# Loading k and v by one 128-partition DMA with three tokens per run, and the difference of the choice in SBUF

## The chip, the cores and the metric

The kernel runs on one core of one Trainium2 chip. The metric is the device time of one execution in microseconds. Engines are named as in the profile: PE (matmul) and PEld (its weight loads), DVE, ACT, POOL, and SP, which issues most of the DMAs.

## The reference

Attention with normalised q and k over 8 batches of 12 heads, 448 tokens and a head width of 64, then a routed layer of 8 experts on the 3584 tokens.

```
q_n, k_n = rmsnorm(q, g_q), rmsnorm(k, g_k)
attn = softmax(q_n @ k_n.T / 8)            # per head, 448 x 448
x = (attn @ v) as (3584, 768)
y_dense = relu(x @ w1_dense) @ w2_dense
logits = x @ w_gate                        # 8 experts
e = argmax(logits); gate = softmax(logits)[e]
out = y_dense + gate * (relu(x @ w1[e]) @ w2[e])
```

All inputs are float32; the matmuls are done in bfloat16.

## The kernel before, in words

**Groups and periods.** The work of attention is cut into 24 groups of four heads (two pairs; three groups make a batch). `first()` fills the pipeline, then `period(g)` (L663) runs once for each of 23 groups, and `final()` ends attention and runs the expert stage (32 tiles of 128 tokens with gathered records). The order of all engines' work is written out by hand: `PLAN` (L642) lists, for each of the three groups of a batch, short names that `period` turns into calls. Each engine works through its instructions in that order.

**What a group goes through.** `load` (L196) brings q, k and v of a group to SBUF; q and k are issued in period g for group g+5 (`Lq`, `Lk`), v for group g+4 (`Lv`). `squares` (L225) squares q and k, on POOL for all but the first groups (L239); `sums` (L241) adds the squares on DVE (L244); `norms` (L248) makes 1/rms on ACT; `normalise` (L271) multiplies, q and half of k on DVE (L285, L282), the other half of k on POOL (L279). `transposes` (L287) turns them on PE (L295), and `turned` (L298) copies the result on DVE (L301 for q, L306 for k). `values` (L219) casts v to bfloat16 on POOL (L221), with a column of ones behind each half. `scores` (L309) does q times k on PE (L319) and the exponential on ACT (L321). `single` (L323, L335) and `attend` (L339, L344) multiply the exponentials with v; `divide` (L348) divides on DVE. `xtrans` (L359, L365) turns the result on PE for the layer that follows. In period g, squares are made for group g+3 and normalising is done for g+2.

**Layout of k and v.** A pair of heads has 7 slots of 64 columns. Slots 0 to 2 are the first head on 128 partitions, slots 4 to 6 the second head, and slot 3 holds the first head's rest on partitions 0 to 63 and the second head's rest on 64 to 127. So 448 tokens of each head are 3.5 slots. Before, this is loaded by four DMAs (L215): for each of the two heads of a pair 256 tokens, four in a run of 1,024 bytes, onto one half of the partitions, and 192 tokens, three in a run of 768 bytes, onto the other half; each DMA covers both pairs. q is loaded by one DMA (L208) of 128 partitions with seven tokens in a run (1,792 bytes), since its slots are permuted back later.

**Buffers and queues.** The q and k buffers (`lds`, three groups deep, L177) lie in the memory of the last two experts' weights, which are loaded when the last groups are done with them; in the profile these loads are `we<-in_q_dram` and `we<-in_k_dram`. v has two buffers (`xv`). SP issues the loads in order q, k, v. In `first()`, ACT's queue issues the second head's pieces of k for groups 0 and 1, ahead of ACT's table load (L749). As the program is built, the loads of SP and ACT use eight completion semaphores in turn, so every load waits until the eighth load before it has landed. The weights go by POOL's queue (`weights`, L631), a few per period, and so do the records of routed tokens (`scatter`, L590).

**The choice of an expert.** Once per batch `logits` (L374) writes 32 numbers a partition to PSUM, and `choose` (L384) picks the largest on DVE: the maximum (L390), the difference to it (L391, into PSUM), a product of "difference is zero" and a priority (L392), its maximum (L395), and the comparison that gives the one-hot choice (L397). `egates` (L407) takes the exponential of the difference on ACT (L409), from PSUM; `gates` (L411) sums and inverts. The PSUM tile is the one that `single` opens anew in the next group (L335).

`lanes` (L152) is some small constant work in `first()` that goes back and forth between DVE (L155 to L160) and POOL (L157, L158).

Of the kernel before, what the change touches and what calls it, by code (L numbers as in the profile page):

```python
# [9 lines left out]
F32 = mybir.dt.float32  # L10
# [3 lines left out]
ALU = mybir.AluOpType  # L14
# [4 lines left out]
def kernel(  # L19
# [14 lines left out]
    nc = tc.nc  # L34
    P = 128
    B, H, S, D = q.shape
    N = B * S
    Dm = H * D
    E = moe_w_gate.shape[1]
    F = moe_w1_dense.shape[1]  # L40
    J = 7
# [7 lines left out]
    De = D + 2  # L49
# [113 lines left out]
    with tc.tile_pool(name="a_ld", bufs=2) as ld, \  # L163
# [13 lines left out]
        lds = [lflat[:, i * 4 * S:(i + 1) * 4 * S].bitcast(F32) for i in range(6)]  # L177
# [18 lines left out]
        def load(g, names="qkv"):  # L196
            if g >= NG:
                return
            for name in names:
                src = dict(q=q, k=k, v=v)[name].rearrange("b h s d -> (b h) s d")[4 * g:4 * g + 4]  # L200
                if name == "v":
                    x = ld.tile([P, 2 * J * D], F32, tag="xv", name="xv")
                else:
                    x = lds[g % 3 * 2 + "qk".index(name)]
                xin[name, g] = x
                xi = x.rearrange("p (i s) -> p i s", i=2)
                if name == "q":
                    nc.sync.dma_start(xi, src.rearrange("(i r) (p j) d -> (r p) i (j d)", r=2, j=J))  # L208
                    continue
                heads = src.rearrange("(i r) s d -> r i s d", r=2)  # L210
                for r in range(2):
                    for c, s0, half in ((4, 0, r), (3, 4 * D, 1 - r)):
                        eng = nc.scalar if g < 2 and name == "k" and r else nc.sync
                        o = (0 if r == 0 else J - c) * D
                        eng.dma_start(xi[half * D:(half + 1) * D, :, o:o + c * D],  # L215
                                      heads[r, :, s0:s0 + c * D]
                                      .rearrange("i (p c) d -> p i (c d)", c=c))
# [7 lines left out]
        def squares(g, name, scalar=False, hs=slice(0, 2)):  # L225
            if (name, g) not in sqs:
                if g == 2:

                    n = "qk".index(name) * 2 * J * D
                    sqs[name, g] = (rall[:, 8:12].rearrange("p m c -> p (m c)")  # L230
                                    [:, n:n + 2 * J * D])
                else:
                    sqs[name, g] = sb.tile([P, 2 * J * D], F32, tag="sq", name="sq", bufs=2)
            o = slice(hs.start * J * D, hs.stop * J * D)
            x, y = xin[name, g][:, o], sqs[name, g][:, o]
            if scalar:
                nc.scalar.activation(y, x, AF.Square)  # L237
            else:
                nc.gpsimd.tensor_mul(y, x, x)  # L239
# [31 lines left out]
        def normalise(g, name, part):  # L271
# [4 lines left out]
            x = xin[name, g].rearrange("p (h j d) -> p h j d", h=2, d=D)  # L276
# [46 lines left out]
        def single(g, hh):  # L323
# [8 lines left out]
            for m in range(4):  # L332
                for r in range(GP):
                    rows = slice(r * D, (r + 1) * D)
                    nc.tensor.matmul(av[:, r, m], exs[g, 3][rows, hh, QC[m]:QC[m] + P],  # L335
                                     vabs[g % 3][rows, hh * J + 3, :De], start=(m == 0), stop=False,
                                     skip_group_check=True)

        def attend(g, hh, ms):  # L339
            av = avs[hh][:, :, :4 * De].rearrange("p r (m e) -> p r m e", e=De)  # L340
            for m in ms:
                for r in range(GP):
                    for j in range(4 * r, 4 * r + 3):
                        nc.tensor.matmul(av[:, r, m], exs[g, j][:, hh, QC[m]:QC[m] + P],  # L344
                                         vabs[g % 3][:, hh * J + j, :De], start=False,
# [38 lines left out]
        def choose(b):  # L384

            ws = trs["w"]
            lp, hot, cent = [ws[:, i * 4 * E:(i + 1) * 4 * E].rearrange("p (m e) -> p m e", e=E)
                             for i in range(3)]
            mx = sb.tile([P, 4, 1], F32, tag="mx", name="mx")
            nc.vector.tensor_reduce(mx, lp, AX.X, ALU.max)  # L390
            nc.vector.tensor_sub(cent, lp, mx.to_broadcast([P, 4, E]))  # L391
            nc.vector.scalar_tensor_tensor(hot, in0=cent, scalar=0.0,  # L392
                                           in1=prio, op0=ALU.is_equal, op1=ALU.mult)
# [599 lines left out]
```

## Time and profile before

| what | value |
|---|---|
| three runs | 401.67, 404.77, 410.85 us |
| median | 404.77 us |
| the profiled execution | 403.7 us, its span 402.0 us |
| PE busy | 341.9 us (85%) |
| PEld, DVE, ACT, POOL busy | 201.2, 225.2, 223.6, 212.3 us |
| DMA | 80.43 MB in 93,493 packets |
| mean granted clock of PE | 0.958 |

Times in the profile are microseconds from the start of the span; in rows of groups the mean is in ns. A row of the timeline has its start, its length, the engine, the line of the code, the operation, what it writes and reads, and how many were merged; square brackets show how long the engine stood idle before it and what ended that. A row of a wait has the sum of the idle time, how often, and the longest. In rows of stretches, DMA share is the busy time of the sixteen DMA engines over the length of the stretch; it can pass 1 a little where packets overlap.

### The profile page before, as it was taken

What the parts mean: (1) busy time and instruction counts of PE and PEld (TensorE: products, weight loads), DVE (VectorE), ACT (ScalarE), POOL (GpSimd) and SP (SyncE); (2) the same over time, 40 slices, a digit from 0 to 9 for tenths busy, and PEclk for the clock granted to TensorE, in tenths of its full rate; (3) what the DMA queues carried; (4) which work ended last, traced back from release to release, by engine and by line L of the source; (5) the groups of instructions that cost most, each with busy time, mean ns of one, the idle gap of its engine ahead of it and who ended that gap; (6) DMA issues with size and microseconds to landing.
All of it is one profiled execution on the core that took longest, in us unless ns stands there. A gap on an engine that the chain in (4) does not pass through costs nothing. (4 is left out here: it accounts for less than half of the span.)

```text
span 402.0 us, 10379 instructions
## 1 busy us (share of the span) xinstructions
PE 341.9 (85%) x3737; PEld 201.2 (50%) x3799; DVE 225.2 (56%) x455; ACT 223.6 (56%) x353; POOL 212.3 (53%) x222
## 2 busy tenths in 40 slices
PE   7589779789789788887988997999999999989940
PEld 3245545445455545544555564455555555545520
DVE  4689779769778777787788553712121212212210
ACT  4579858768778768678868752323233332322300
POOL 6686485966885776577887413544522121211220
PEclk9989989899999989899989998999999999999995
DMA  8979989999998989787999899999867867657530
GB/s 213 239 179 221 243 205 231 248 262 235 277 241 207 255 223 243 244 185 235 232 219 238 190 209 198 202 236 213 214 153 156 195 126 127 138 130 189 133 118 0
DMA packets 93493, 80.43 MB, mean 200 GB/s; under 512 B 53754, under 2 KB 84986, under 8 KB 93440
## 3 DMA queue, kind: packets, MB, share of 16 engines
q1 hardware_dynamic: 81360, 43.45, 49.7%
q0 software_dynamic: 11504, 35.81, 35.5%
q8 instruction: 34, 0.56, 0.6%
q10 hardware_dynamic: 576, 0.46, 0.4%
q14 instruction: 19, 0.16, 0.1%
HBM read 61.40 MB, written 26.19 MB: 218 GB/s over the span
## 5 line engine op out<-in xcount | busy, mean ns | idle before, releaser
L321 ACT ACTIVATE exf<-sc 128x896 bf16<-128x896 f32 x168 | 150.4, 916 | 47.7 <-PE sc L319 43.0
L239 POOL TENSOR_TENSOR sq<-we 128x896 f32<-128x896 f32 (+1 forms) x43 | 72.3, 1682 | 8.7 <-DMA we<-in_q_dram 3.2
L319 PE MATMUL sc<-T 64*128 64x448 bf16 (+1 forms) x384 | 63.4, 375 | 15.4 <-ACT exf L321 12.5
L591 POOL DMA_INDIRECT records<-rall,slot x32 | 33.0, 1032 | 47.4 <-issue 12.7
L853 ACT COPY heT<-hp 128x512 bf16<-128x512 bf16 x32 | 18.7, 586 | 66.7 <-PE hp L851 66.7
L244 DVE TENSOR_REDUCE ssq<-sq 128x14 f32<-128x896 f32 (+1 forms) x48 | 49.6, 1039 | 8.2 <-ACT sq L237 4.3
L344 PE MATMUL av<-va,exf 128*128 128x66 bf16 x1152 | 53.5, 197 | 0.0
L870 DVE COPY exf<-yp 128x768 f32<-128x768 f32 x20 | 19.2, 958 | 59.1 <-PE yp L864 52.7
L871 POOL DMA_INDIRECT out_dram<-exf,tail x20 | 19.6, 979 | 55.0 <-DVE exf L870 55.0
L344 PEld LDWEIGHTS <-exf 128*128 128x128 bf16 x1152 | 41.8, 99 | 12.3 <-issue 9.7
L839 PE MATMUL he<-we,exf 128*128 x177 | 44.3, 385 | 3.5 <-DMA exf<-records 1.6
L859 PE MATMUL yp<-wd,exf 128*128 128x384 bf16 x256 | 46.8, 326 | 0.0
L864 PE MATMUL yp<-we,heT 128*128 x256 | 46.8, 326 | 0.0
L319 PEld LDWEIGHTS <-T 64*128 64x128 bf16 (+1 forms) x384 | 17.9, 96 | 54.0 <-issue 47.0
L609 PE MATMUL ff<-wd,xT 128*128 128x512 bf16 x117 | 41.3, 398 | 1.0 <-issue 0.3
L844 ACT ACTIVATE hs<-he,tail 128x512 bf16<-128x512 f32 x32 | 22.0, 687 | 27.0 <-PE he L839 22.8
L859 PEld LDWEIGHTS <-exf 128*128 128x128 bf16 x256 | 25.0, 98 | 19.7
L354 DVE TENSOR_TENSOR rall<-av,inv 128x512 bf16<-128x512 f32 x48 | 33.2, 692 | 1.7
L870 DVE COPY rall<-yp 128x768 f32<-128x768 f32 x12 | 11.5, 958 | 39.5 <-PE yp L864 39.5
L864 PEld LDWEIGHTS <-heT 128*128 128x128 bf16 x256 | 25.0, 98 | 16.6
L279 POOL TENSOR_TENSOR xn<-we,r 128x448 bf16<-128x448 f32 x25 | 23.8, 953 | 16.0 <-ACT r L269 9.8
L871 POOL DMA_INDIRECT out_dram<-rall,tail x12 | 11.8, 979 | 35.4 <-DVE rall L870 35.4
(160 smaller groups left out, 441.9 us busy)
## 6 DMA issues: line engine op xcount, KB each, us to landing
we<-in_moe_w_dram POOLq DMA_DIRECT2D x16, 768.0 KB
we<-in_q_dram SPq DMA_DIRECT2D x24, 448.0 KB
xv<-in_v_dram SPq DMA_DIRECT2D x48, 128.0 KB
we<-in_k_dram SPq DMA_DIRECT2D x46, 128.0 KB
xv<-in_v_dram SPq DMA_DIRECT2D x48, 96.0 KB
we<-in_k_dram SPq DMA_DIRECT2D x46, 96.0 KB
wd<-in_moe_w_dense_dram POOLq DMA_DIRECT2D x2, 768.0 KB
exf<-records SPq DMA_TRANSPOSE x64
```

What stands on the lines that cost most here:

```text
L239: nc.gpsimd.tensor_mul(y, x, x)
L244: nc.vector.tensor_reduce(ssqs[g][:, "qk".index(name), hs], sqs[name, g].rearrange("p (h j d) -> p h j d", h=2, d=D)[:, hs], AX.X, ALU.add)
L319: nc.tensor.matmul(ps[o, hh, :S], kT[rows, j * P + o.start:j * P + o.stop], qT[rows, r * S:(r + 1) * S], start=True, stop=True)
L321: nc.scalar.activation(x, ps[:, :, :S], AF.Exp, scale=scale)
L344: nc.tensor.matmul(av[:, r, m], exs[g, j][:, hh, QC[m]:QC[m] + P], vabs[g % 3][:, hh * J + j, :De], start=False, stop=(j == 4 * r + 2), sk ...
L354: nc.vector.tensor_mul(xas[b].rearrange("p m a c -> p (m a) c")[:, :, o:o + D] .rearrange("p n (r d) -> p r n d", r=2), av[:, :, :, :Dh], ...
L591: i = nc.gpsimd.indirect_dma_start(out=rec, out_offset=bass.IndirectOffsetOnAxis(ap=slot[b % 2][:, m:m + 1], axis=0), in_=rb[b % 3][:, m], ...
L609: nc.tensor.matmul(ff[0], xTs[b][:, kk, QC[m]:QC[m] + P], wd1[:, kk], start=(kk == 0), stop=(kk == KD - 1))
L839: nc.tensor.matmul(he, xRs[t][:, kk % 2 * 5 + kk // 2], we[:, :n][:, bass.ds(eregs[t], 1), 0, kk * F:(kk + 1) * F] .rearrange("p o f -> p ...
L859: nc.tensor.matmul(yp[:, dd, :HD], xRs[t][:, i // 2 * 5 + 3 + i % 2], wd2[:, i, dd * HD:(dd + 1) * HD], start=(i == 0), stop=False)
L864: nc.tensor.matmul(yp[:, dd, :HD], heTs[t][:, i], we[:, :EA if t < KA else E][:, bass.ds(eregs[t], 1), 1, i * Dm + dd * HD:i * Dm + (dd + ...
L871: i = nc.gpsimd.indirect_dma_start(out=out, out_offset=bass.IndirectOffsetOnAxis(ap=tail[:, t, 1:2], axis=0), in_=ys.rearrange("p a d -> p ...
```

## The change

k and v are loaded by three DMAs in place of four. One covers 128 partitions and takes the first 384 tokens of all four heads, three in a run (768 bytes, four runs a partition). Two small ones cover 64 partitions each and take the last 64 tokens of each head, one in a run (256 bytes), into the shared slot. All are issued by SP, the first groups' too. For that, k's buffer grows from 14 to 16 slots, with one unused slot behind each pair, so that k is read as two runs of 448 numbers; v's slots are put in another order, the four heads' three slots first and the shared ones last, and `vslot` gives the matmuls the place. In `choose` the difference goes to a tile in SBUF, and "is the largest" is found by comparing the logits with the maximum, in an operation of its own before the product with the priority: six DVE operations in place of five. ACT takes the exponential from the SBUF tile.

```diff
-        lds = [lflat[:, i * 4 * S:(i + 1) * 4 * S].bitcast(F32) for i in range(6)]
+        WQ, WK = 2 * J * D, 16 * D
+        lds = [lflat[:, 2 * o:2 * (o + w)].bitcast(F32) for i in range(3)
+               for o, w in ((i * (WQ + WK), WQ), (i * (WQ + WK) + WQ, WK))]
...
                 if name == "v":
-                    x = ld.tile([P, 2 * J * D], F32, tag="xv", name="xv")
+                    x = ld.tile([P, WQ], F32, tag="xv", name="xv")
+                    xin[name, g] = x
+                    a, c = x[:, :12 * D], x[:, 12 * D:].rearrange("p (i d) -> p i d", i=2)
                 else:
                     x = lds[g % 3 * 2 + "qk".index(name)]
-                xin[name, g] = x
-                xi = x.rearrange("p (i s) -> p i s", i=2)
+                    xi = x.rearrange("p (i s) -> p i s", i=2)
+                    xin[name, g] = xi[:, :, :J * D]
+                    a, c = x, xi[:, :, 3 * D:4 * D]
...
-                heads = src.rearrange("(i r) s d -> r i s d", r=2)
+                nc.sync.dma_start(a.rearrange("p (n x) -> p n x", n=4)[:, :, :3 * D],
+                                  src[:, :3 * P].rearrange("n (p c) d -> p n (c d)", c=3))
                 for r in range(2):
-                    for c, s0, half in ((4, 0, r), (3, 4 * D, 1 - r)):
-                        eng = nc.scalar if g < 2 and name == "k" and r else nc.sync
-                        o = (0 if r == 0 else J - c) * D
-                        eng.dma_start(xi[half * D:(half + 1) * D, :, o:o + c * D],
-                                      heads[r, :, s0:s0 + c * D]
-                                      .rearrange("i (p c) d -> p i (c d)", c=c))
+                    nc.sync.dma_start(c[r * D:(r + 1) * D],
+                                      src[:, 3 * P:].rearrange("(i r) p d -> r p i d", r=2)[r])
+
+        def vslot(i, j):
+            return 12 + i if j == 3 else 6 * i + j - j // 4
...
-            o = slice(hs.start * J * D, hs.stop * J * D)
-            x, y = xin[name, g][:, o], sqs[name, g][:, o]
+            x = xin[name, g][:, hs]
+            y = sqs[name, g].rearrange("p (h s) -> p h s", h=2)[:, hs]
...
-                                     vabs[g % 3][rows, hh * J + 3, :De], start=(m == 0), stop=False,
+                                     vabs[g % 3][rows, vslot(hh, 3), :De], start=(m == 0), stop=False,
...
-            lp, hot, cent = [ws[:, i * 4 * E:(i + 1) * 4 * E].rearrange("p (m e) -> p m e", e=E)
-                             for i in range(3)]
+            lp, hot = [ws[:, i * 4 * E:(i + 1) * 4 * E].rearrange("p (m e) -> p m e", e=E)
+                       for i in range(2)]
+            cent = sb.tile([P, 4, E], F32, tag="cent", name="cent", bufs=1)
...
-            nc.vector.scalar_tensor_tensor(hot, in0=cent, scalar=0.0,
-                                           in1=prio, op0=ALU.is_equal, op1=ALU.mult)
+            nc.vector.scalar_tensor_tensor(hot, in0=lp, scalar=0.0, in1=mx.to_broadcast([P, 4, E]),
+                                           op0=ALU.add, op1=ALU.is_equal)
+            nc.vector.scalar_tensor_tensor(hot, in0=hot, scalar=1.0, in1=prio, op0=ALU.mult,
+                                           op1=ALU.mult)
```

4 lines of the change are left out of this document (2 added, 2 removed).

## The prediction

> **What bounds the kernel now.** I read the page's header and DMA rows first, then the busy times by stretch, then SP's timeline and waits, and last the timeline around each stall of TensorE.
>
> ```profile
> span 402.0 us, 10379 instructions
> q1 hardware_dynamic: 81360, 43.45, 49.7%
> q10 hardware_dynamic: 576, 0.46, 0.4%
> ```
>
> ```profile
> 30.00:130.00 100.00, 84.65 (x1275) 52.43 (x1291) 82.55 (x152) 78.84 (x124) 69.98 (x61) 0.97 1.01 237
> 130.00:200.00 70.00, 58.77 (x854) 35.62 (x869) 53.48 (x99) 53.37 (x87) 51.73 (x47) 0.95 0.92 230
> 257.00:380.00 123.00, 120.70 (x756) 70.68 (x770) 29.20 (x38) 36.96 (x59) 36.34 (x38) 1.00 0.77 171
> ```
>
> The columns are length, busy PE, PEld, DVE, ACT, POOL, clock, DMA share and GB/s. The expert stage (257 to 380) is PE's own: 120.70 of 123 us busy; nothing in this change touches it. In the attention stage PE is busy 143.4 of 170 us, and the sixteen DMA engines are full (1.01 and 0.92) at only 230 to 237 GB/s. So there is no slack in the DMA engines, but a late load costs time only where PE ends up waiting for it. I looked for these places.
>
> First place, the start:
>
> ```profile
> 9.26 0.51 SPq L208 DMA_DIRECT2D we<-in_q_dram  x1
> 13.98 1.68 POOL L239 TENSOR_TENSOR rall<-we 128x896 f32<-128x896 f32 x1 [3.29 <-DMA we<-in_q_dram]
> 16.14 0.16 DVE L159 TENSOR_REDUCE lw<-lw 128x1 f32<-128x8 f32 x1 [2.03 <-POOL lw L158]
> 16.34 1.00 DVE L160 TENSOR_SCALAR lane<-lane,lw 128x8 f32<-128x8 f32 x1
> 17.25 1.07 DVE L285 TENSOR_TENSOR xn<-we,tq 128x896 bf16<-128x896 f32 x1
> 18.91 0.55 PE L295 MATMUL tq<-ident,xn 128*128 128x128 bf16 x7 [2.68 <-DVE xn L282]
> ```
>
> The third q (group 2) is issued at 9.26, POOL squares it at 13.98 after 3.29 us of waiting, the small lane work queues behind that on POOL, DVE stands 2.03 us for it, and PE stands 2.68 us for DVE. Second and third place, groups 5 and 6:
>
> ```profile
> 38.81 1.67 POOL L239 TENSOR_TENSOR sq<-we 128x896 f32<-128x896 f32 x1 [3.23 <-DMA we<-in_q_dram]
> 42.25 0.61 PE L365 MATMUL tx<-ident,rall 128*128 128x128 bf16 x8 [0.56 <-DVE T L301]
> 49.19 1.68 POOL L239 TENSOR_TENSOR sq<-we 128x896 f32<-128x896 f32 x1 [2.65 <-PE av L344]
> 50.91 1.09 DVE L244 TENSOR_REDUCE ssq<-sq 128x14 f32<-128x896 f32 x1 [3.26 <-POOL sq L239]
> 51.91 0.68 DVE L301 TENSOR_SCALAR T<-tq,gqk 128x896 bf16<-128x896 bf16 x1
> 52.64 0.61 PE L365 MATMUL tx<-ident,rall 128*128 128x128 bf16 x8 [3.21 <-DVE T L301]
> ```
>
> At 49.19 the row names PE, but a square reads only the loaded q and writes a free buffer; I take the wait to be q of group 6, issued at 40.01 (below). The chain is square, sum (3.26 us), the turned copy queued behind the sum on DVE, and PE stands 3.21 us.
>
> **Why those loads are late.** SP's queue and its waits between 30 and 280 us:
>
> ```profile
> 29.23 0.54 SPq L208 DMA_DIRECT2D we<-in_q_dram  x1
> 29.88 3.12 SPq L215 DMA_DIRECT2D we<-in_k_dram  x4
> 33.09 6.18 SPq L215 DMA_DIRECT2D xv<-in_v_dram  x4
> 39.32 0.59 SPq L719 DMA_DIRECT2D records<-rall  x1
> 40.01 0.38 SPq L208 DMA_DIRECT2D we<-in_q_dram  x1
> ```
>
> ```profile
> SPq L215 <- DMA we<-in_q_dram: 14.6, 8, 3.7
> ```
>
> A group is nine DMAs, and each waits for the eighth before it; so the last piece of v waits for q of its own group. That is the 6.18 us at 33.09, the 14.6 us in eight waits, and it holds q of group 6, whose buffer DVE had freed some 7 us earlier, until 40.01.
>
> And the transfers are slow when they are halves:
>
> ```profile
> 8.00:9.00 1.00, 0.52 (x3) 0.29 (x2) 1.00 (x3) 0.33 (x2) 1.00 (x2) 1.00 1.13 194
> 9.00:10.00 1.00, 0.66 (x9) 0.52 (x9) 0.69 (x3) 0.65 (x4) 0.46 (x2) 1.00 1.13 247
> 10.00:11.00 1.00, 0.58 (x7) 0.26 (x6) 0.80 (x2) 1.00 (x2) 0.69 (x1) 1.00 1.22 193
> 11.00:12.00 1.00, 0.74 (x8) 0.25 (x5) 0.65 (x2) 0.35 (x1) 0.00 (x0) 1.00 0.86 288
> 17.00:18.00 1.00, 0.00 (x0) 0.00 (x0) 1.00 (x2) 0.09 (x1) 1.00 (x2) 1.00 0.93 291
> 47.00:49.00 2.00, 2.00 (x43) 1.56 (x42) 0.64 (x2) 1.86 (x3) 0.00 (x0) 1.00 1.10 207
> ```
>
> From 8 to 11 and 47 to 49 pieces of k and v (64 partitions each) are in flight: full engines, 193 to 247 GB/s, mean of the four rows 210. At 11 to 12 and 17 to 18, some 2 us after a q was issued, mostly q (128 partitions) is: 288 and 291.
>
> **The change, part by part.**
>
> *Transfer of k and v.* A load stays 458,752 bytes. Now 512 packets of 768 and 1,024 bytes; then 512 of 768 and 256 of 256. If halves are the cause, it goes from 458,752/210 = 2.2 us to 458,752/290 = 1.6 us. If the shorter runs are (q's are 1,792 bytes), 50% more packets make it 3.3 us. The q10 row decides: ACT's four early pieces of k are packets of the same 768 and 1,024 bytes, and 0.46 MB took 0.4% of 16 times 402 us, 25.7 us, which is 17.9 GB/s an engine or 286 GB/s on sixteen. So such packets are not slow in themselves, and I take 1.6 us, plus 0.1 to 0.3 for the small ones.
>
> *Issue on SP.* Seven DMAs in place of nine per group. A q took 0.51 and four pieces 2.55 us (0.64 each); I take 0.5 to 0.65 for the big one, as q is the nearest, and 0.64 for a small one: 1.9 for 2.55 us. If 512 runs took twice a q's time it is 2.3, still less. The eighth DMA before now lies in the group before, so v no longer waits for its own q. ACT loses four issues; its table load moves up, which hides behind the wait for the first q. SP takes over the two early halves of k, so the second q is issued about 0.5 us later, covered by engines that still have k of group 0 to move.
>
> *The start.* Up to its third q 2.75 MB have to land. Three q at 290 and three k or v at 1.7 us are 4.7 + 5.1 = 9.8 us against 13.98 - 1.9 - 0.8 = 11.3 us in which they came (first bytes at 1.9 and 0.8 from the last byte to its use, read from the trace's packet records, which no view lists). That is 1.5 us; with SP issuing that q near 7.8, and the second k no longer held for a semaphore, I take 1.9, between 1.0 and 2.6. PE's 2.68 us there cover all of it.
>
> *Groups 5 and 6.* q of group 5 is issued 3 to 5 us earlier (SP is no longer behind), q of group 6 near 33 in place of 40. POOL needed them 3.23 and 2.65 us earlier than it had them, so both stalls go: 0.56 and 3.21 us of PE. Next late after that is v (a cast, used two groups later). Ends: 0 (weights fill the engines anyway) and 3.8.
>
> *Squares of k* now read two runs of 448 with a gap. A square of one half took longer than half:
>
> ```profile
> L239 POOL TENSOR_TENSOR sq<-we 128x896 f32<-128x896 f32 x42 | 71.4, 1700 | 6.9 <-DMA we<-in_q_dram 3.2 <-PE av L344 2.7 <-ACT exf L321 0.9
> L239 POOL TENSOR_TENSOR sq<-we 128x448 f32<-128x448 f32 x1 | 0.9, 934 | 1.8 <-DMA we<-in_k_dram 1.8
> ```
>
> Twice 934 is 168 ns over 1,700: from 0 to 0.17 us each. POOL is idle about 28% of the attention stage, which hides it; I take 0. The new order of v's slots changes addresses alone.
>
> *The choice.* One more DVE operation per batch, and the difference lies in SBUF:
>
> ```profile
> 87.65 0.20 DVE L392 SCALAR_TENSOR_TENSOR av<-av,prio 128x32 f32<-128x32 f32 x1
> 88.11 0.19 DVE L397 SCALAR_TENSOR_TENSOR oh<-av,m 128x32 bf16<-128x32 f32 x1
> 88.22 1.08 DVE L285 TENSOR_TENSOR xn<-we,tq 128x896 bf16<-128x896 f32 x1
> 88.58 0.30 PE L335 MATMUL av<-va,exf 64*128 64x66 bf16 x8 [0.88 <-ACT eg L409]
> 89.88 0.33 PE L295 MATMUL tq<-ident,xn 128*128 128x128 bf16 x3 [0.52 <-DVE xn L282]
> ```
>
> PE no longer waits for ACT's exponential at 88.58 but for the choice, 0.1 to 0.3 us sooner. It gains nothing: 1.3 us later it stands 0.52 us for DVE, and the operations behind the choice start later by 0.11 (L397 to L285, the pitch of independent ones) to 0.23 us (L392 to the next but one, halved). Six such batches: 0.7 to 1.4 us lost, I take 1.0. The choice of the last batch lies beside dense matmuls.
>
> *Sum.* -1.9 - 0.6 - 3.2 + 1.0 = -4.7 us. The profiled run took 403.7 us (span 402.0), 1.07 under the median 404.77. So 399.0 us.
>
> **Rivals.** *Nothing is gained on PE* (chance 0.20): weights and records fill the engines as before and the stall of group 6 only moves to group 7. Against it stands the free buffer at 33; for it the share of 1.01. Only the start's 1.0 and the choice's 1.0 are left: 403.7.
>
> *Slower: the small runs* (0.09). If every packet costs alike, a load takes 3.3 for 2.2 us, 2.2 us more per group. The engines are full over some 18 groups from 30 to 200 us; if half of it reaches PE, 20 us: about 423. It decides from 0.45 us per group that PE sees (8.1 us in 18 groups, 2% of 404.77). The q10 row speaks against it. The Trainium skill says so too in "DMA: Bandwidth & Descriptors", Specifications: runs under 512 bytes miss line rate, because they are read and modified; no row here shows a 256-byte load. By that rule the 256 small packets might count double, an estimate of some 0.3 us per load on top of 1.7, still under 2.2.
>
> *More than forecast* (0.19). The three runs spread by 9.2 us (401.67 to 410.85). If that spread is late loads, the new median lies near the floor: 401.67 - 5.7 = 396.
>
> **Chances and range.** The forecast has 0.52, 396.5 to 402. 2% is 8.1 us, about what a measurement of this kernel can tell from no change: under 396.7 lie most of the third rival (0.16) and a part of the forecast (0.14), so faster 0.30; slower 0.09; same 0.61. The range runs from 394, the third rival less 2 us, to 406, the first plus 2; outside lie 0.09 above and 0.08 below.
>
> **What would show it.** Right: 768-byte loads at 280 GB/s or more with full engines; no wait of SP's v for its own q; POOL's squares at the three places without a wait, and PE's 2.68 and 3.21 us gone. Wrong: DMA share above 1 at under 230 GB/s from 30 to 130 us; a big DMA that holds SP over 1 us; a new wait of squares for k; PE's 0.52 us per batch grown to over 0.8.

## The result, and the profile after

| | before | after |
|---|---|---|
| median of the runs | 404.09 us (401.67 to 410.85, 4 runs) | 390.25 us (387.48 to 390.91, 4 runs) |
| ratio, 95% interval | | 0.9664 [0.9589, 0.9738] |
| profiled execution: time, span | 403.7, 402.0 | 389.9, 388.2 |

The changed kernel is faster by 3.4%. The forecast was 399.0 us, with a range of 394 to 406, and faster by 2% or more had a chance of 0.30: the way was forecast, the size was not, and 390.25 lies below the range. Ratios here are formed from a kernel's runs within 1.5% of its fastest; the times of this program spread more than that from execution to execution, so medians over all runs stand beside them.

The page of the changed kernel, and the same two stretches as before (length, busy PE, PEld, DVE, ACT, POOL, clock, DMA share, GB/s):

```profile
span 388.2 us, 10370 instructions
q1 hardware_dynamic: 93456, 43.90, 50.7%
```

```profile
30.00:130.00 100.00, 93.92 (x1435) 56.80 (x1434) 90.31 (x172) 86.83 (x139) 79.40 (x70) 1.00 0.99 261
130.00:200.00 70.00, 65.82 (x1006) 39.47 (x1001) 63.06 (x121) 59.99 (x95) 57.10 (x53) 1.00 0.99 246
```

TensorE is busy 159.7 of 170 us where it had 143.4, and full DMA engines move 261 and 246 GB/s where they moved 237 and 230. Next the places of the prediction: SP's queue, then the third square, then TensorE behind it.

```profile
7.65 0.59 SPq L213 DMA_DIRECT2D we<-in_q_dram  x1
24.29 0.54 SPq L213 DMA_DIRECT2D we<-in_q_dram  x1
28.32 2.06 SPq L218 DMA_DIRECT2D xv<-in_v_dram  x2
31.18 0.60 SPq L213 DMA_DIRECT2D we<-in_q_dram  x1
```

```profile
11.97 1.68 POOL L244 TENSOR_TENSOR rall<-we 128x896 f32<-128x896 f32 x1 [1.62 <-DMA we<-in_q_dram]
```

```profile
17.14 0.55 PE L300 MATMUL tq<-ident,xn 128*128 128x128 bf16 x7 [1.25 <-DVE xn L287]
```

The third q leaves SP at 7.65 (9.26 before), q of group 5 at 24.29 (29.23), q of group 6 at 31.18 (40.01). In this profile the third square starts 2 us sooner, and TensorE's wait there is 1.25 for 2.68 us; most later profiles do not repeat that (see the start, below). The waits of 0.56 and 3.21 us for the turned copy in groups 5 and 6 have shrunk to one of 0.3:

```profile
PE tx L370 <- DVE T L306: 0.3, 1, 0.3
```

But one wait in this profile is new. TensorE's waits from 215 to 235 us (in all, times, longest):

```profile
PE he L847 <- DMA exf<-records: 13.9, 2, 11.6
```

At the end of attention it stands 13.9 us for the first records of the experts' part, where before it stood 1.15 us at that place. Attention had become some 25 us shorter, and half of that was given back here. That is far more than three early stalls, and a second profile of each kernel shows why it must not be read as the change's doing alone.

### Two executions of each kernel

The first row is VectorE's division (`divide`, `d1`) at the end of a period in the kernel before, the second the same instruction in the changed one:

```profile
104.09 0.26 DVE L352 RECIPROCAL inv<-av 128x16 f32<-128x16 f32 x1 [1.72 <-PE sc L319]
```

```profile
92.78 0.26 DVE L357 RECIPROCAL inv<-av 128x16 f32<-128x16 f32 x1
```

In the first, TensorE's last product for it had ended at 102.30, but its semaphore (the signal that tells a waiting engine of the end) came at 104.07; in the second the division starts 0.04 us after the product. In the profile before this happens in two of three periods: VectorE waits 1.7 to 2.0 us there, ScalarE's exponential waits too, and in one of the two TensorE then stands 1.3 to 1.7 us for that. I call such an execution *late*, the other *prompt*. A second profile of the unaltered changed kernel (a2_again) is late, a second one of the kernel before (b2_again) prompt. So this does not belong to the change.

It does not look like chance from one execution to the next either: the 18 later profiles were taken in six series, each a set of kernels run on one chip one after the other, and within a series all are of one kind. Kernels 1 to 4 below are late, a2_again and kernels 6 to 8 late, 12 late, 13 and 14 late; kernels 9, 10 and b2_again are prompt, and so are 15 to 18, on the same chip as 1 to 4. The late profiles also lack records: of TensorE's semaphore increments they hold 468 to 477, the prompt ones 499 to 506. Whether unprofiled runs are late at all is therefore not known.

The table takes, from each trace, the second division of a period ("end of period"), the second product of the experts' part (L839 or L847) and the span:

| profile | loads | completions | end of period 3 | 5 | 23 | experts' 2nd product | span |
|---|---|---|---|---|---|---|---|
| before | old | late | 57.2 | 75.1 | 241.9 | 244.9 | 402.0 |
| a2_again | new | late | 52.8 | 70.0 | 233.5 | 236.3 | 393.0 |
| b2_again | old | prompt | 57.8 | 74.8 | 232.4 | 247.4 | 403.9 |
| after | new | prompt | 50.8 | 67.0 | 216.2 | 232.4 | 388.2 |

Read down the pairs. By period 5 the new loads lead by 5.1 us among the late and 7.8 among the prompt ones. From period 5 to 23 the late pair takes 166.8 and 163.5 us, the prompt pair 157.6 and 149.2. In this table a prompt execution runs through attention 9.5 to 17 us sooner and then waits 12 to 13 us more for the first records (15.0 and 16.2 us from period 23 to the second product, for 3.0 and 2.8), so the spans of one kernel lie close together. At the experts' part the lead is 8.6 us (late) and 15.0 us (prompt); the medians differ by 13.8. The pairs join profiles of different series, so their differences hold that of the series too.

### The profile page after: what moved, and what is told of

Its sections match the earlier page's. It is cut to its first block, busy times and chain, and to the rows that moved or that the text cites. A ratio compares the mean times of both kernels' runs of the same rounds, so it can differ in the third digit from the quotient of the medians.

```text
span 388.2 us, 10370 instructions
## 1 busy us (share of the span) xinstructions
PE 341.6 (88%) x3799; PEld 198.0 (51%) x3799; DVE 224.9 (58%) x463; ACT 221.7 (57%) x353; POOL 212.1 (55%) x222
## 3 DMA queue, kind: packets, MB, share of 16 engines
q0 software_dynamic: 11504, 35.81, 36.5%
## 4 chain that ended last, share of the span: by engine, by line
PE 52%; DMA 22%; POOL 6%; DVE 6%; issue 4%; SPq 3%; ACT 3%; POOLq 0%; DVEq 0%; ACTq 0%
PE he L847 11%; DMA xv<-in_v_dram 11%; PE yp L872 11%; PE yp L867 11%; DMA we<-in_k_dram 6%; DMA exf<-records 5%; PE sc L324 4%; PE av L349 4%; POOL sq L244 3%; PE ff L617 2%; PE hp L859 2%; DVE ssq L249 2%; SPq L218 2%; ACT exf L326 2%; POOL xn L284 2%
## 5 line engine op out<-in xcount | busy, mean ns | idle before, releaser
L324 PE MATMUL sc<-T 64*128 64x448 bf16 (+1 forms) x384 | 61.9, 364 | 4.0 <-ACT exf L326 3.5
L847 PE MATMUL he<-we,exf 128*128 x192 | 48.1, 387 | 13.9 <-DMA exf<-records 13.9
L861 ACT COPY heT<-hp 128x512 bf16<-128x512 bf16 x32 | 18.7, 585 | 66.1 <-PE hp L859 66.1
L349 PE MATMUL av<-va,exf 128*128 128x66 bf16 x1152 | 52.6, 194 | 0.0
L617 PE MATMUL ff<-wd,xT 128*128 128x512 bf16 x156 | 50.7, 381 | 0.0
L349 PEld LDWEIGHTS <-exf 128*128 128x128 bf16 x1152 | 41.2, 97 | 11.7 <-issue 9.2
L867 PEld LDWEIGHTS <-exf 128*128 128x128 bf16 x256 | 25.0, 98 | 19.7
L847 PEld LDWEIGHTS <-exf 128*128 128x128 bf16 x192 | 17.7, 99 | 30.2 <-DMA exf<-records 14.5
L284 POOL TENSOR_TENSOR xn<-we,r 128x448 bf16<-128x448 f32 x25 | 23.9, 956 | 13.6 <-ACT r L274 12.1
```

The source lines that it names most:

```text
L284: nc.gpsimd.tensor_mul(y[:, 0], x[:, 0], rs["s", g][:, n].unsqueeze(2) .to_broadcast([P, J, D]))
L324: nc.tensor.matmul(ps[o, hh, :S], kT[rows, j * P + o.start:j * P + o.stop], qT[rows, r * S:(r + 1) * S], start=True, stop=True)
L617: nc.tensor.matmul(ff[0], xTs[b][:, kk, QC[m]:QC[m] + P], wd1[:, kk], start=(kk == 0), stop=(kk == KD - 1))
L847: nc.tensor.matmul(he, xRs[t][:, kk % 2 * 5 + kk // 2], we[:, :n][:, bass.ds(eregs[t], 1), 0, kk * F:(kk + 1) * F] .rearrange("p o f -> p ...
L867: nc.tensor.matmul(yp[:, dd, :HD], xRs[t][:, i // 2 * 5 + 3 + i % 2], wd2[:, i, dd * HD:(dd + 1) * HD], start=(i == 0), stop=False)
```

## The experiments

Short names: *old loads* are those before the change, *new loads* those after; "choose" is the routing step whose difference went from PSUM to SBUF.

**1 and 2. Each part alone.** Kernel 1 is before with the new `choose`; kernel 2 is after with the old one.

```
-            cent = sb.tile([P, 4, E], F32, tag="cent", name="cent", bufs=1)
...
-            nc.vector.scalar_tensor_tensor(hot, in0=lp, scalar=0.0, in1=mx.to_broadcast([P, 4, E]),
-                                           op0=ALU.add, op1=ALU.is_equal)
-            nc.vector.scalar_tensor_tensor(hot, in0=hot, scalar=1.0, in1=prio, op0=ALU.mult,
-                                           op1=ALU.mult)
+            nc.vector.scalar_tensor_tensor(hot, in0=cent, scalar=0.0,
+                                           in1=prio, op0=ALU.is_equal, op1=ALU.mult)
```

This is kernel 2, whose `cent` is again the third slice of the PSUM bank; kernel 1 has the same lines the other way round.

> The kernel before with the new choose alone (difference in SBUF, one more VectorE operation); the loads are the old ones. Theory A (the steady gain of some 16 us between 50 us and the end of attention is choose's: with the difference in PSUM, ScalarE's exponential of it kept the bank that the next single() writes, PE waited 0.84 to 0.91 us for eg in each of 6 batches, and the 1.3 to 1.7 us waits of the scores for exf beside it follow from the same bank): about 404 - 6 x 2.5 = 389 to 394 us, PE's waits for eg gone and those for exf at 76, 105, 133, 162, 191 and 220 us gone. Theory B (it is the loads'): 403 to 405 us, PE's waits for exf still there, only the 0.9 us for eg gone.

> The changed kernel with the old choose (difference in PSUM); the loads are the new ones. Theory A: 398 to 400 us, that is the start and the stalls of groups 5 and 6 alone (5.7 us), with PE's waits for eg and exf back in each batch. Theory B: 389 to 392 us, at most the 0.9 us for eg in each of 6 batches above the changed kernel, PE's busy time in 30 to 130 us near 93 of 100.

Measured: 407.71 us (398.75 to 410.14) for `choose` alone, beside 403.56 for the kernel before in the same series; 390.72 us (387.75 to 393.57) for the loads alone, ratio 0.9676 [0.9536, 0.9816]. Theory A falls, the gain is the loads'. Its 0.9 and 1.5 us waits turned up in both profiles, because both are late in most batches: what I had taken for a trace of `choose` was one of late profiles. That `choose` alone is 4 us slower by the medians lies within the spread of the runs; the fastest are 398.75 and 398.86.

**3 and 4. Partitions or number of DMAs.** After with each big DMA cut in two, once by partitions and once by heads:

```
-                nc.sync.dma_start(a.rearrange("p (n x) -> p n x", n=4)[:, :, :3 * D],
-                                  src[:, :3 * P].rearrange("n (p c) d -> p n (c d)", c=3))
+                for u in (slice(0, D), slice(D, P)):
+                    nc.sync.dma_start(a.rearrange("p (n x) -> p n x", n=4)[u, :, :3 * D],
+                                      src[:, :3 * P].rearrange("n (p c) d -> p n (c d)", c=3)[u])
```

Kernel 4 has `for u in (slice(0, 2), slice(2, 4))` in its place and takes `[:, u]` on both sides.

> The changed kernel with each big DMA of k and v cut into two of 64 partitions (the same runs of 768 bytes, 9 DMAs for a group of q, k and v as before the change). If it is the 128 partitions of one DMA that bring the throughput (261 against 237 GB/s in 30 to 130 us): back to about 237 GB/s and 400 us or more. If it is the smaller number of DMAs, with their issue time and their waits for a completion semaphore: 397 to 400 us, and the cut by pairs of heads is as slow. If neither: 390 us.

> The changed kernel with each big DMA of k and v cut into two by heads (two heads each, all 128 partitions, runs of 768 bytes, 9 DMAs for a group). If the 128 partitions of one DMA matter: 390 us, unlike the cut by partitions. If the number of DMAs matters: 397 to 400 us, like the cut by partitions. If neither: 390 us in both.

Measured: 410.07 us (401.61 to 419.27) by partitions, 396.42 (394.86 to 399.99) by heads, with 403.56 for the kernel before. Same bytes, same runs, same nine DMAs; by the medians the halves cost 13.7 us, by each kernel's runs within 1.5% of its fastest 6.5. The rows of 30 to 130 us, kernel 3 and kernel 4:

```profile
30.00:130.00 100.00, 83.30 (x1235) 52.06 (x1251) 80.13 (x149) 75.83 (x122) 69.41 (x61) 0.95 1.01 229
```

```profile
30.00:130.00 100.00, 84.26 (x1303) 52.93 (x1322) 85.79 (x159) 81.79 (x130) 74.70 (x66) 1.00 0.94 248
```

With halves the engines are full at 229 GB/s; whole, they move 248 and are not full. In the packet records of the same stretch a 768-byte packet takes 55 ns in kernel 3 and 53 in the kernel before, 41 ns in kernel 4 and after. The Trainium skill has the rule in "DMA: Bandwidth & Descriptors", Rules for kernel authors: two transfers to disjoint halves of the partitions gain nothing, use one of 128. By that rule, the trace agrees, and here they even cost. The number of DMAs counts too: nine against seven is 396.42 against 390.72 (kernel 2, same series).

**5. The changed kernel again**, unaltered.

> The changed kernel once more, unaltered. In its first profile TensorE's completions reached VectorE and ScalarE at once and attention ended near 217 us; in the profiles of before and of the four kernels above they come up to 1.9 us late at two places of each batch. If this prompt state belongs to the kernel: the waits of 1.3 to 1.7 us for exf stay away, the last norms stand near 195 us, the wait for the first records is again about 11 us. If it belongs to the single execution: they are back, the last norms stand near 208 us, the wait for the records is 1 to 3 us, and the time is again 388 to 391 us, because what TensorE gains in attention is given back at the records.

Measured: 394.68 us, one run, late; TensorE's waits before the experts' part are these (225 to 245 us):

```profile
PE he L847 <- issue: 0.9, 1, 0.9
```

The prompt state does not belong to the kernel, and with it the long wait for the records is gone. The time is a little above the expected 388 to 391.

**6 and 7. Late weights.** After, and kernel 2, with the last three expert weights issued beside the first tile:

```
-            return {NG - 5: 15, NG - 4: 16}.get(g, len(wjobs))
+            return {NG - 5: 15}.get(g, 16)
...
                if t < P // 16:
                    gap(t)
+               if t == 0:
+                   weights(len(wjobs))
```

> The changed kernel with the last three expert weights (jobs 16 to 18, 2.36 MB) issued by GpSimd after the first tile of the experts' part in place of the period before the last; no tile before the ninth reads them. Theory C (after attention the DMA engines are the bound: they are full to 229 us and the first records wait behind these weights): 2.36 MB at some 250 GB/s, 9 us, leave the stretch of 206 to 229 us, the waits of 11.6 and 2.4 us for the records shrink to 2 to 5, 380 to 384 us. Theory D (the wait is not the weights' but the transposes' own time or the listing's, and attention is in truth as slow as in the kernel with the old choose): 388 to 392 us.

> The same late weights with the old choose (difference in PSUM) and the new loads. If the old choose makes attention 12 us longer, as its profile showed, and the records hid that in the end: 388 to 391 us, 8 us above the late weights with the new choose. If the difference of the two profiles was one of executions: within 2 us of the late weights with the new choose.

Measured: 404.73 us (400.79 to 410.2) and 405.49 (401.39 to 409.5). Both miss: TensorE waits 4.72 and 6.94 us at 273.81 and 281.32 (4.65 and 6.75 in kernel 7). The rows name records, not the weights; by the packet records GpSimd's queue, with the moved weights, takes from 256 to 276 us 0.82 to 0.99 of the DMA engines' time. So the edit seems only to have moved a cost. Both profiles are late, so Theory C, meant for the wait of a prompt one, stays untested. The second question is answered: the two `choose` differ by 0.8 us, less than the runs spread.

**8. The small DMAs the other way.**

```
-   for r in range(2):
-       nc.sync.dma_start(c[r * D:(r + 1) * D], src[:, 3 * P:].rearrange("(i r) p d -> r p i d", r=2)[r])
+   for i in range(2):
+       nc.sync.dma_start(c[:, i], src[2 * i:2 * i + 2, 3 * P:])
```

> The changed kernel with the two small DMAs of k and v cut the other way: each takes one pair of heads, 128 partitions with one run of 256 bytes, in place of 64 partitions with two. If a DMA of 64 partitions is what costs (768-byte packets of 54 ns against 41 ns in the cuts above): the 256-byte packets of 19 ns get quicker and the time falls by 1 to 3 us, to 387 to 389. If only the large transfers feel it: 390 us.

Measured: 437.9 us (437.12 to 445.54), ratio 1.0891 [1.0772, 1.1009], the largest miss of the study, and by way of a resource I had not thought of. While small DMAs are in flight (170 of the 207 load packets from 100 to 102 us are of 256 bytes):

```profile
100.00:101.00 1.00, 1.00 (x20) 0.65 (x17) 1.00 (x2) 0.39 (x1) 0.40 (x1) 1.00 0.15 39
101.00:102.00 1.00, 1.00 (x15) 0.60 (x13) 0.97 (x3) 0.90 (x2) 1.00 (x1) 1.00 0.16 33
```

A share of 0.15 is 2.4 of 16 engines. A packet takes 20 ns as before; but the first pair of these DMAs lasts 1.9 us for its 256 packets, and 0.7 us in the changed kernel. Behind them v's big DMA and the next q hold SP 1.6 to 3.5 us each from 93 to 110 us. The Trainium skill says it in "DMA: Bandwidth & Descriptors", Rules for kernel authors: the outermost dimension sets how many engines a DMA uses, and a dimension of 2 confines it to at most two. By that rule, the trace agrees; 128 partitions on the SBUF side did not help where the pattern starts with two heads.

**9 and 10. New loads for a part of the groups** (`NEW(g)` is `g < 7` or `g >= 7`; the others are loaded by the lines of before; new `choose` in both).

> The changed kernel with the new k and v loads for groups 0 to 6 alone; groups 7 to 23 are loaded as before, by two DMAs of four and two of three tokens on 64 partitions each. Theory E (the gain is that of the first 57 us, as the prediction summed it, and the rest is the chance of half-clock windows in single executions): 390 to 393 us. Theory F (the old loads also cost later, where they fill the DMA engines: 54 ns for a 768-byte packet against 41): about 404 - 5.5 = 398 to 400 us.

> The other half: groups 0 to 6 loaded as before, 7 to 23 by the new loads. Theory E: 402 to 405 us, the time before. Theory F: 396 to 399 us, some 6 to 8 us below before, with PE's waits for tx at 42 and 53 us as before and fewer waits behind loads from 60 us on.

Measured: 393.99 us (388.66 to 403.97) for the first seven groups, 395.08 (392.21 to 397.11, ten runs) for the other seventeen; the kernel before has 405.64 (394.93 to 409.45) in the series. By the medians each half brings more than 10 us and both together 14; by the fastest runs alone kernel 10's ratio is 0.9949 [0.9884, 1.0015]. Theory E's 402 to 405 for the later groups alone is missed by all ten runs, but two of the thirteen runs of the kernel before (394.93 and 396.08) lie as low, so the times alone do not settle it.

The profiles, both prompt and in one series with b2_again, separate the two parts. The end of period 5 stands at 69.1 us (new loads first), 73.8 (old loads first) and 74.8 (b2_again); from there to period 23 it takes 159.5 us (old loads), 148.8 (new loads) and 157.6 (b2_again). So the later loads are worth 9 to 11 us of attention, which the prediction had not priced. At the experts' second product the three stand at 232.8, 235.9 and 247.4 us: each part alone brings most of what the whole change brings there (232.4 in the profile after), because TensorE then waits for the first records, 2.0 us in kernel 9, 11.0 in kernel 10, 12.7 in b2_again. What is won in attention does not simply add up in the time.

**11. The kernel before again**, unaltered.

> The kernel before once more, unaltered, for what of its profile returns: by the prediction the waits of 2.7, 0.6 and 3.2 us at 19, 42 and 53 us. Theory E: the half-clock windows after 60 us stand elsewhere or are fewer, and no load is late after 60 us. Theory F: from 60 us on there are waits behind late loads in this execution too (as in the profile with the new choose alone at 109 us, 2.5, and at 227 us, 3.7).

Measured: 405.6 us, one run, prompt. The early waits return (2.47 us at 18.54, 3.56 at 52.63), and Theory F holds. TensorE's waits from 60 to 230 us, b2_again first, then after, the prompt pair:

```profile
PE tx L365 <- DVE T L301: 8.1, 7, 4.3
PE tq L295 <- DVE xn L282: 3.6, 11, 0.5
PE sc L319 <- ACT exf L321: 3.2, 7, 0.6
```

```profile
PE tq L300 <- DVE xn L287: 5.1, 11, 0.7
PE sc L324 <- ACT exf L326: 1.3, 6, 0.2
PE tx L370 <- DVE T L306: 1.3, 3, 0.6
```

The 8.1 against 1.3 us for the turned copy is most of the 8.4 us by which the old loads take longer from period 5 to 23 (157.6 and 149.2). One wait makes up 4.35 of the 8.1; the other six are of 0.2 to 1.2 us and were not followed back to a load. The long one, engine by engine (POOL, DVE, PE):

```profile
199.56 0.98 POOL L221 CAST va<-xv 128x896 bf16<-128x896 f32 x1 [4.30 <-DMA xv<-in_v_dram]
202.42 1.71 POOL L239 TENSOR_TENSOR sq<-we 128x896 f32<-128x896 f32 x1
```

```profile
204.17 1.09 DVE L244 TENSOR_REDUCE ssq<-sq 128x14 f32<-128x896 f32 x1 [4.53 <-POOL sq L239]
205.18 0.68 DVE L301 TENSOR_SCALAR T<-tq,gqk 128x896 bf16<-128x896 bf16 x1
```

```profile
205.90 1.01 PE L365 MATMUL tx<-ident,rall 128*128 128x128 bf16 x8 [4.35 <-DVE T L301]
```

A late v holds POOL 4.30 us in its cast, three weight issues and the square stand behind it in POOL's order though the square's q has landed, the sum waits for the square, the turned copy behind the sum, and TensorE stands 4.35 us. POOL's waits for v in the whole stretch, b2_again and after:

```profile
POOL va L221 <- DMA xv<-in_v_dram: 13.0, 5, 4.3
```

```profile
POOL va L226 <- DMA xv<-in_v_dram: 4.2, 1, 4.2
```

**12 and 13. Fewer weights.** Before and after, each with three of 18 large weight DMAs left out:

```
                if nw[0] < len(wjobs):
-                    nc.gpsimd.dma_start(*wjobs[nw[0]])
+                    if not 12 <= nw[0] < 15:
+                        nc.gpsimd.dma_start(*wjobs[nw[0]])
...
+                    if g in (8, 10, 12):
+                        nc.vector.memset(wjobs[8 + g // 2][0], 0.0)
```

> The kernel before, with its old loads and old choose, but three of the 18 large weight DMAs are left out (the second matrix of expert 4 and both of expert 5; VectorE writes zeros in their place earlier), so the experts' part computes something else. Theory G (the DMA engines' time up to the first expert product sets the end: it was 237.5 and 245.9 us per engine in the two profiles before, 219.4 and 227.8 in the two of the changed kernel, 18 less in both pairs): the weights took 77.6 us per engine for 18, so 13 us leave the sum without any change to the k and v loads, and the time falls by 9 to 13 us, to 391 to 396, with the first product of the experts at 232 to 236 us. Theory H (the gain is in the loads themselves, by when they land for the first groups and by what 64-partition writes do to the other engines): 402 to 406 us, as before.

> The changed kernel with three of the 18 large weight DMAs left out (the second matrix of expert 4 and both of expert 5; VectorE writes zeros in their place earlier), so the experts' part computes something else; the counterpart of the same cut in the kernel before, which brought 1 us. Theory G: with the new loads the DMA sum falls to some 206 to 215 us and is no bound at all; what stays is attention's own chain, so 386 to 390 us at most 4 below the changed kernel, and the spread of the runs gets smaller. Theory H: 390 to 391 us.

Measured: 400.06 us (398.18 to 404.09) beside 401.34 for the kernel before, ratio 1.0043 [0.9966, 1.012]; and 394.5 (390.12 to 396.7) beside 400.3, ratio 0.9867 [0.9776, 0.9959]. Theory G misses twice: the DMA engines' time per engine to the first expert product fell to 223.4 and 207.3 us, and the end did not follow. Theory H (402 to 406, and 390 to 391) is missed as well, by 2 and 3.5 us on either side; that kernel 13 lies above the changed kernel is not explained. Both profiles are late, with 164.1 and 160.7 us from period 5 to 23.

**14. More weights.** After, with three weight DMAs issued twice:

```
+                    if g in (8, 12, 16):
+                        nc.gpsimd.dma_start(*wjobs[g // 2 - 1])
```

> The changed kernel with three weight DMAs of 768 KB issued a second time, spread over attention (jobs 3, 5 and 7 again, in periods 8, 12 and 16), so that the DMA engines have 13 us each more to do (77.6 us for 18 of them before) and nothing else changes. Theory G (the DMA engines' time up to the first expert product sets the end in some executions, attention's own chain of work on the engines in others, and the later of the two counts): the sum rises from 219 to 228 us to 232 to 241, as before the change, and the time by 5 to 13 us, to 396 to 403. Theory H (the DMA sum does not count, only when the first groups' loads land): 390 to 392 us.

Measured: 384.66 us (382.75 to 391.13): more work and 5.6 us less than the changed kernel, where neither theory had it. In the late profile the experts' second product stands at 233.5; what got shorter is the time from the last product to the end, 6.8 us for 15.2. Of these 8.4 us 6.9 are GpSimd's last DRAIN, 0.81 us where it took 7.67 in all profiles with 93 DMAs on its queue.

**15 to 18. Is it the number of GpSimd's DMAs?** After with three, two and one additional DMAs of 12 KB into a spare tile, and before with three:

```
+    junk = const.tile([P, KD, E], BF16)
...
+                    if g in (8, 12, 16):
+                        nc.gpsimd.dma_start(chunk_pairs(junk), two_rows(moe_w_gate))
```

> The changed kernel with three more DMAs on GpSimd's queue that move next to nothing (12 KB of the gate's weights into a spare tile, in periods 8, 12 and 16). GpSimd's last DRAIN took 7.67 us in each profile with 93 DMAs on its queue, 7.42 with 90, and 0.81 with 96. If the number of DMAs on that queue sets it: 0.8 us, the program ends about 7 us sooner after the last product (6.8 us in place of 15.2) and the time is 382 to 385 us. If the bytes or descriptors of the three large DMAs did it: 7.7 us or more, 389 to 392 us; then the large re-issue also hid some cost of its DMA time.

> Two such small DMAs, 95 on GpSimd's queue. By the number: the DRAIN is either 7.8 us (it grows by 0.08 us for one DMA and falls back at 96) or below 1 us (it falls back sooner). By the bytes: 7.7.

> One such small DMA, 94 on GpSimd's queue. By the number: 7.75 us, or below 1 if it falls back here. By the bytes: 7.7.

> The kernel before with three such small DMAs, 96 on GpSimd's queue. By the number: its last DRAIN falls to 0.8 us and its time by some 7 us, to 394 to 398; this gain has nothing to do with the k and v loads, so the changed kernel with the same three keeps its lead of 10 to 14 us. By the bytes: 401 to 405 us.

Measured: 382.4 us (372.91 to 384.51), 382.59 and 387.6 (one run each), and 392.91 (386.73 to 396.53) for before with three, beside 403.42. SP's wait for the other engines at the end, after and then kernel 15:

```profile
SPq L996 <- PEq L996: 7.7, 2, 7.1
```

```profile
SPq L999 <- PEq L999: 1.2, 2, 0.7
```

Bytes do not decide: with 94, 95 and 96 DMAs the DRAIN takes 0.73, 0.97 and 1.22 us, with 93 it takes 7.67. The number of DMAs alone does not either, as 96 gave 0.81 in kernel 14 and 1.22 in kernel 15. In the order of the packets of that queue (q0 on the page) it falls back once: 10,816 packets 7.42 us, 11,504 packets 7.67, 11,904 packets 0.73, 11,936 (kernel 14) 0.81, 12,304 packets 0.97, 12,704 packets 1.22. Kernel 15 beats both kernels (two small DMAs were as quick in one run). Beside it experiment 14, also with 96 DMAs and with 13 us more of DMA time, is 2.3 us slower (384.66 against 382.4, from two series). And it gives a third pair for the loads: 392.91 against 382.4, 10.5 us, the second expert product at 245.5 and 233.1 in two prompt profiles.

## Why the prediction was right in part and wrong in size

**The transfer.** Right. From the packet records of 30 to 130 us a load was 256 x 53 + 256 x 70 ns over 16 engines, 1.97 us (forecast from the rows: 2.2), and is 512 x 41 + 256 x 19 ns, 1.62 us (forecast 1.6, plus 0.1 to 0.3 for the small pieces). The halves were the cause, as kernels 3 and 4 show. The q10 row could not decide that: ACT's early pieces of k were halves of 64 partitions themselves and by that working moved at 286 GB/s all the same, so the row spoke against the shorter runs and as much against the halves. That the conclusion held is luck. The rival of slow small runs falls: a 256-byte packet took 19 ns, 0.30 us of a load. The Trainium skill's rule of 512 bytes, in "DMA: Bandwidth & Descriptors", Specifications, shows as 13.5 bytes per ns against 18.7 for the 768-byte packets, and no more than that.

**Issue on SP.** Right. Third q at 7.65 (forecast 7.8), group 6's at 31.18 (33), a big DMA 0.37 to 0.6 us as long as no semaphore holds it, and v's wait for its own q, 14.6 us in eight waits, is this row from 30 to 280 us:

```profile
SPq L215 <- DMA we<-in_q_dram: 0.2, 1, 0.2
```

**The start**, -1.9 us. It came out in the first profile and, of the others, only in kernel 14's, so that agreement was luck. SP issues the third q at 7.6 us in all eleven profiles with the new loads in the first groups, for 8.9 in the mean of the six with the old ones (kernels 3, 4 and 8 belong to neither). But the third square starts at 13.2 us in the mean of the eleven (11.8 to 14.2) and at 13.6 in that of the six (13.3 to 14.0), and the end of period 0 stands at 29.7 and 30.0. So the term was 0.3 us, below its range of 1.0 to 2.6; why the earlier issue brings so little there is open.

**Groups 5 and 6**, -0.6 and -3.2, together -3.8 us. Right, if a little small: over the same profiles the lead grows from 0.3 us at the end of period 0 to 5.0 at the end of period 3 (52.3 for 57.3), and at the end of period 5 it is 5.5 (69.1 for 74.7). With the start they were to bring 5.7; the sum fits because one is too large and the other too small.

**The choice**, +1.0 us. The mechanism was right, the size too large. In the late profile a2_again the wait for the exponential has become one for the choice, 0.71 to 0.78 for 0.84 to 0.91 us, and the wait that follows grew from 0.52 to 0.75:

```profile
110.05 0.30 PE L340 MATMUL av<-va,exf 64*128 64x66 bf16 x8 [0.77 <-DVE oh L405]
111.57 0.55 PE L300 MATMUL tq<-ident,xn 128*128 128x128 bf16 x7 [0.75 <-DVE xn L287]
```

That is some 0.1 us net for a batch, 0.6 for six. Kernel 2 against the changed one (390.72 and 390.25) shows nothing of it.

**Where it failed** is the sentence "Next late after that is v (a cast, used two groups later)", which priced v, and with it every load after group 6, at nothing. The cast may be two groups ahead, but it stands in POOL's order ahead of squares and of half of k's normalising that are not. The profile of the kernel before has one named wait of this kind, and no wait of TensorE over 0.2 us stands in the ten us after it:

```profile
64.09 1.00 POOL L221 CAST va<-xv 128x896 bf16<-128x896 f32 x1 [4.13 <-DMA xv<-in_v_dram]
```

In b2_again a wait as long reached TensorE through the square and the sum (4.30, 4.53, 4.35 above). In kernel 9, with old loads from group 7 on, a longer one held half of k's normalising, two scatters of records and a weight issue behind it, and TensorE stood 5.21 us for that (POOL, PE):

```profile
206.64 0.97 POOL L244 CAST va<-xv 128x896 bf16<-128x896 f32 x1 [7.75 <-DMA xv<-in_v_dram]
212.07 0.93 PE L318 MATMUL tk<-ident,xn 128*128 128x128 bf16 x7 [5.21 <-POOL xn L302]
```

So a late v costs what stands behind its cast just then, and a profile in which it cost nothing is no price for the next.

The size, from the end of period 5 to that of period 23: in the prompt profiles 155.8 to 159.5 us with old loads there (b2_again, kernels 9 and 18) and 148.8 to 149.7 with new ones (after, kernels 10 and 15 to 17), 8.4 us between the means and no overlap. Of this the way through v is traced for the 4.35 and 5.21 us alone. In the late ones it is 164.1 to 169.8 (before, kernels 1 and 12) and 160.7 to 166.4 (seven with new loads), 3.6 us between the means, with an overlap; in the one late series with both, kernel 1 takes 169.8 and kernels 2 and 4 take 162.4 and 162.0, which is 7.6. So the term that was left out is 4 to 8 us of attention. With 5.5 by period 5 and the choice at zero the sum is 9 to 14; measured were 8.6 and 15.0 in the pairs and 13.8 in the medians. That is a sum over attention. How it reaches the end of a prompt execution, where TensorE may wait some 13 us for the records after attention, stays open.

**The third rival**, more than forecast at 0.19, was the case in kind; its 396 us was still too high. Its ground, that the spread of the runs is late loads, is not shown: ten runs of kernel 10 lie within 4.9 us and thirteen of the kernel before within 14.5, but kernels 6 and 7, with new loads as well, spread by 9.4 and 8.1.

**Left open.** Why completions come late in some series is not settled, nor whether unprofiled runs have it. Neither is the wait of a prompt execution for its first records, 12.7 us in b2_again and 13.9 in the profile after, but 2.0 in kernel 9: kernels 6 and 7, meant for it, were late. And the DMA engines' time, 18 us less per engine to the first expert product in both pairs (237.5 to 219.4, 245.9 to 227.8), is an effect of the change, but experiments 12 to 14 do not show it as a bound: with 13 us less of it the time hardly moved.

## What to carry to other kernels

Count the partitions and the outer dimension of a load ahead of the length of its runs: here the same 768-byte packet took 53 to 55 ns in loads of 64 partitions and 41 ns in loads of 128, and small loads that began with a dimension of two kept 2.4 of 16 engines busy. When a wait behind a load costs nothing in a profile, ask what stands behind its reader in the reader's order, and what the same wait would cost a little earlier or later. Before a sum is built on the waits of one profile, take a second one of the unaltered kernel: here it would have shown v's price, and several of the changed kernel showed that the gain of 1.9 us at the start was one profile's.

## What the runs showed of the hardware that was not expected

- Semaphore increments of TensorE came up to 2.0 us after the end of the product, several within 0.15 us of each other, at the same two places of each batch, in twelve of the twenty profiles. The first such wait of VectorE stands anywhere from 70 us (kernel 2) to 116 us (kernel 3). In the stretch before 104.07 us of the profile before two increments of ScalarE are on record and came at once; three others of ScalarE and two of VectorE have no record. Whether the profiling itself has a part in this is open.
- The granted clock fell to half for stretches of 3.41 us or a multiple, within some 3 us after gaps of TensorE of 0.7 to 3.2 us. In the profile before, three periods take 27.57 us without such a stretch (104.09 to 131.66) and 28.95 to 29.45 with one, so one costs about 1.5 us. The Trainium skill has this window of 3413 ns, free-running, in "TensorE: Matmul & The Clock Gate", Part 1; by that rule, the trace agrees in the length. Like gaps brought a stretch at some places and none at others: kernels 6 and 7 had three and four between 100 and 190 us, kernels 2 and 13 none, though kernel 2 has three gaps of 1.4 to 1.5 us there.
- GpSimd's DRAIN at the end took 7.42 and 7.67 us with 10,816 and 11,504 packets on its queue and 0.73 to 1.22 us with 11,904 to 12,704. Why it falls back is open.
